# Gathered keys and queries turned at group 12 instead of 2, and batch 1's values loaded straight into their tile

## The chip, the cores and the metric

The kernel runs on one core of one Trainium2 chip. The time is what the device takes for one execution, in microseconds (us). The engines named here: PE (TensorE) does matrix products, and PEld is its loading of weights; DVE (VectorE) and ACT (ScalarE) work on tiles; POOL (GpSimd) makes small copies and issues those DMAs that also change the data's type; SP (SyncE) issues the other DMAs. Each engine takes its instructions in the order in which the program gives them, so an instruction that waits holds up all that is behind it on its engine.

## The reference

Eight batches, eight heads, 576 positions, heads of 64. Each query sees the keys within 32 positions; 8 given global positions are seen by all and see all. The attention's output, one row of 512 per position, goes through two layers with a "snake" between them.

```python
scores = scale * np.matmul(q, k.transpose(0, 1, 3, 2))
mask = np.abs(pos[:, None] - pos[None, :]) <= window
mask = mask | is_global[:, None] | is_global[None, :]
attn = softmax(np.where(mask, scores, -1e9))
x = (attn @ v).transpose(0, 2, 1, 3).reshape(B * S, H * D)
h = x @ w_in
g = h + np.sin(alpha * h) ** 2 / (alpha + 1e-09)
out = g @ w_out
```

## The kernel before, in words

The work goes batch by batch, in an order written out by hand. For each batch there is an attention (`attention`, line 831) and a GEMM 1 with the snake (`gemm1`, line 1126); GEMM 2 of a batch (`gemm2`) is a queue of single products, from which `fill(n)` takes n at given places of the following attention and GEMM 1, so that PE has work there. The order is: attention 0, GEMM 1 of batch 0, attention 1 with GEMM 2 of batch 0 in it, GEMM 1 of batch 1, and so on.

**GEMM 1** has 16 groups (`nt`). Each takes 8 products of PE into one of three PSUM banks (zn, zr, zd in turn), then `sb` = sin on ACT (line 1187), its square `s2` on ACT (1190) or DVE (1192), and H on DVE (1193), which frees the bank. In GEMM 1 of batch 0, PE also turns batch 1's keys and queries head by head (`turn_lying`, groups 4, 7, 10 and 13, into the banks zo), and DVE and ACT put them in their places one group later (`place_lying`, groups 5, 8, 11 and 14, lines 685 and 692).

**The global keys and queries** of all batches are gathered by 16 small DMAs of SP (`gather_heads`, line 536), cast on POOL in group 1 (`cast_globals_kq`, line 766, first keys, then queries), turned by 32 small products of PE at the end of group 2 (`turn_kq`, line 775, into the bank zo1), and copied by DVE to kTg and qTg (line 780). In group 3 POOL issues the casts of batch 2's keys and queries to DRAM (`cast_qk(2)`, line 337) and copies the globals of batch 1 into its key and query tiles (`place_globals`, three copies, lines 378 and 381), which attention 1's scores read.

**The values** of batches 0 and 1 lie in the tiles VF0 and VF1: two halves of partitions, each with even rows and, from a copy (`odd_rows`, line 415), odd rows beside them; `edge_tiles` (line 421) makes the tile VE of the rows at the edge, two copies for each half. A batch's numerators (`numerators`, products with VF and VE at line 911) need both. Batch 0's values come by 12 DMAs of POOL (line 396) straight from the input. Batch 1's come in two steps: POOL casts them into a DRAM tile `vpd` with one DMA (line 402), and SP loads VF1 from it with two (line 408). For batch 1, POOL makes odd_rows and edge_tiles of the second half in group 3 and DVE those of the first in attention 1.

**POOL's queue** in the beginning, DMAs and casts in order: keys and queries of batch 0, the 12 of values 0, w_in's first half, the cast of the gathered values, keys and queries of batch 1 (first heads), w_in's second half, keys and queries of batch 1 (last heads), w_out's first half, vpd, w_out's second half, the casts of `cast_globals_kq`, and then `cast_qk(2)`.

**Attention 1** goes over four head pairs (`hp`). Each has two halves of scores (line 863), exp on ACT (871) and a mask on DVE (`cover`, 880); `denominators(hp - 1)`, whose logarithm (ACT) comes before the sums GD (DVE, line 805); from hp 2 on `numerators(hp - 2)`, normalised on DVE (954). ACT loads a table for exp at its start (line 838) and one for sin at its end (1031). After each head pair, `beside(hp)` adds work: for batch 1 at 0 the value copies on DVE, `turn_qk(2)` (two transposing DMAs of SP, line 354, from the casts of `cast_qk(2)`), and at 0 and 1 the squares of the batch before (`square_x`, lines 1070 to 1074). `beside(-1)` comes before the first head pair, `beside(4)` after the last has been normalised.

**Batch 2's keys and queries**, once transposed, go to their tiles in eight copies of DVE (`place`, lines 370 and 363), four of keys first; for batch 2 all eight are made in groups 4, 5, 7, 8, 10, 11, 13 and 14 of GEMM 1 of batch 1. For later batches they are made in the attention, in `beside(2)`, `(3)` and `(4)`.

Of the kernel before, what the change touches and what calls it, by code (L numbers as in the profile page):

```python
# [12 lines left out]
DT = mybir.dt  # L13
# [237 lines left out]
def kernel(  # L251
# [11 lines left out]
    nc = tc.nc  # L263
    B, H, S, D = q.shape
# [7 lines left out]
    NH = KT // 2  # L272
    CT = DM // P
    NT = DFF // P
    HALF = S // 2
# [13 lines left out]
    dramp = mctx.enter_context(tc.tile_pool(name="dramp", bufs=2, space=bass.MemoryType.DRAM))  # L289
# [38 lines left out]

    cast = {}
    turned = {}  # L330
    vpd = dramp.tile([HALF, H, 2, D], DT.bfloat16, name="vpd")

    def cast_qk(b):

# [55 lines left out]
            tensor=q0.tensor, offset=q0.offset, ap=[list(q0.ap[0]), [2 * QROW, NHP], [SEG, 7], [1, 4]]  # L390
        )

    def load_v0():
        for half in range(2):
            for m in range(NT6):
                nc.gpsimd.dma_start(
                    out=VF[0][half * D : half * D + NH, m].rearrange("p h y d -> p h (y d)"),
                    in_=v[0].rearrange("h (n m a y) d -> n m a h (y d)", n=2, a=NH, y=2)[half, m],
                )

    def cast_v1():
        nc.gpsimd.dma_start(
            out=vpd[:].rearrange("s h y d -> s h (y d)"), in_=v[1].rearrange("h (s y) d -> s h (y d)", y=2)
        )

    def load_v1():
        for half in range(2):
            nc.sync.dma_start(
                out=VF[1][half * D : half * D + NH].rearrange("p m h y d -> p m (h y d)"),
                in_=vpd[:].rearrange("(n m a) h y d -> n a m (h y d)", n=2, a=NH)[half],  # L410
            )

    def odd_rows(b, half, copy):
        r = half * D
        copy(out=VF[b][r + 32 : r + 32 + NH, :, :, 0], in_=VF[b][r : r + NH, :, :, 1])

    def edge_tiles(b, half, copy):
        r, m = (1 - half) * D, half * (NT6 - 1)
        for y in range(2):
            o = half * D + y * 32  # L420
            copy(out=VE[b][o : o + NH], in_=VF[b][r : r + NH, m, :, y])
# [94 lines left out]
    for t in (gidx8, gp64):  # L516
        nc.vector.memset(t[:].bitcast(DT.int32), 0)
    nc.sync.dma_start(
        out=g64[:],
# [114 lines left out]
        nc.gpsimd.iota(qpos[half * D : half * D + D], pattern=[[KT, NT6], [1, 2], [2, 24]], base=half * HALF,  # L634
                       channel_multiplier=0, allow_small_or_imprecise_dtypes=True)
    gather(v, gv)
    load_v0()
    load_w_in((0,))
    nc.gpsimd.tensor_copy(out=VGb[:], in_=gv.rearrange("p h d -> p (h d)"))
    for hps in (early, late):  # L640
# [2 lines left out]
        if hps == early:  # L643
            load_w_in((1,))
    load_w_out((0,))
    cast_v1()
    load_w_out((1,))
    gather_heads(k, gk)
    gather_heads(q, gq)
# [414 lines left out]
    def square_x(b, part):  # L1064


        W = SG if b == B - 1 else S
        xf = xTs[b][:, :, 0:W]
        if part == 0:
            nc.vector.tensor_tensor(out=SQ[:, :, 0:W], in0=xf, in1=xf, op=ALU.mult)  # L1070
            return
        nc.vector.tensor_tensor(out=SQ[:, 0:2, 0:W], in0=SQ[:, 0:2, 0:W], in1=SQ[:, 2:4, 0:W], op=ALU.add)
        nc.vector.tensor_tensor(out=SQ[:, 0, 0:W], in0=SQ[:, 0, 0:W], in1=SQ[:, 1, 0:W], op=ALU.add)
        nc.vector.tensor_tensor(out=RM[:, 0:W], in0=RM[:, 0:W], in1=SQ[:, 0, 0:W], op=ALU.max)
# [45 lines left out]
    ON_ACT_FIRST = (1, 3, 5, 7, 9, 11, 13, 14)  # L1120
    ON_ACT_SECOND = (1, 3, 5, 7, 9, 10, 12, 13)

    TURNED, PLACED, GLOBALS = (4, 7, 10, 13), (5, 8, 11, 14), 2
    PLACED_LATE = {4: 0, 5: 1, 7: 2, 8: 3, 10: 4, 11: 5, 13: 6, 14: 7}

    def gemm1(b):


        while len(waiting) > 1:
            fill(1)  # L1130
        xT = xTs[b]
        r0 = (b % 2) * S
        more = b == B - 1
        W = SG if more else S
        hr = tc.alloc_tile_pool(name="hr", bufs=1, space=PSUM)
        hs = {}

        def chunks(nt, cs, parts=slice(0, 2)):
            if nt not in hs:
                hs[nt] = (zn, None, zd)[nt % 3] or hr.tile([P, 2, 512], DT.float32, name="zr")  # L1140
            h = hs[nt]
            for c in cs:
                for h_part, lo, hi in halves(h, W)[parts]:
                    nc.tensor.matmul(  # L1144
                        out=h_part, lhsT=w_in[:, c, nt * P : (nt + 1) * P], rhs=xT[:, c, lo:hi],
                        start=(c == 0), stop=(c == CT - 1), skip_group_check=True,
                    )

        on_act = (ON_ACT_FIRST, ON_ACT_SECOND, ON_ACT)[min(b, 2)]
        for nt in range(NT):  # L1150
            at_group[0] = (b, nt)
            if b == 1 and nt in PLACED_LATE:
                place(2, *PLACES[PLACED_LATE[nt]], nc.vector.tensor_copy)
            if b == 0 and nt in PLACED:
                hp = PLACED.index(nt)
                for w, copy in ((1, nc.vector.tensor_copy), (0, nc.scalar.copy)):
                    place_lying(1, w, hp, banks_of[NHP - 1][w], copy)
            if b == 0 and nt == 1:
                lay_global_values(1, zo[0], nc.vector.tensor_copy)
                cast_globals_kq()  # L1160
            if b == 0 and nt == GLOBALS + 1:

                cast_qk(2)
                load_v1()
                for part in range(3):
                    place_globals(1, part, nc.gpsimd.tensor_copy)
                odd_rows(1, 1, nc.gpsimd.tensor_copy)
                edge_tiles(1, 1, nc.gpsimd.tensor_copy)
            if more and nt == SOON:
                put_globals(slice(0, SOON))  # L1170
            if nt == 0:

                for n in range(2):
                    chunks(n, range(CT - 1), slice(0, 2 - more))
                for n in range(2 * more):
                    chunks(n, range(CT - 1), slice(1, 2))
            chunks(nt, range(CT - 1, CT) if nt < 2 else range(CT))
            h = columns(hs[nt], W)
            fill((GROUP_LAST if more else PER_GROUP)[nt])
            if nt and copied[0] == (b, nt - 2):  # L1180
                fill(AFTER_COPY)
            if b == 0 and nt in TURNED:
                turn_lying(1, TURNED.index(nt), banks_of[NHP - 1])
            if b == 0 and nt == GLOBALS:
                turn_kq()
            sb = spool.tile([P, SG], DT.bfloat16, name="sb")
            nc.scalar.activation(out=sb[:, 0:W], in_=h, func=AF.Sin, scale=alphaT[:, nt : nt + 1])  # L1187
            s2 = spool.tile([P, SG], DT.bfloat16, name="s2")
            if nt in on_act:
                nc.scalar.activation(out=s2[:, 0:W], in_=sb[:, 0:W], func=AF.Square)  # L1190
            else:
                nc.vector.tensor_tensor(out=s2[:, 0:W], in0=sb[:, 0:W], in1=sb[:, 0:W], op=ALU.mult)  # L1192
            nc.vector.scalar_tensor_tensor(  # L1193
                out=H2[:, nt, r0 : r0 + W], in0=s2[:, 0:W], scalar=recipT[:, nt : nt + 1], in1=h,
                op0=ALU.mult, op1=ALU.add,
            )
        hr.release()
        at_group[0] = None
# [121 lines left out]
    def places_at(b_att, at):  # L1320
        if b_att + 1 == B:
            return ()
        share = {} if b_att == 1 else {2: (0, 3), 3: (3, 6), 4: (6, 8)}
        return PLACES[slice(*share.get(at, (0, 0)))]

    def phase_a(b_att, b_moe):
        def beside(at):

            if b_att == 0:
                copy = nc.vector.tensor_copy  # L1330
                if at in (0, 2):
                    hp = 2 + at // 2
                    turn_lying(0, hp, banks_of[hp])
                    place_lying(0, 1, hp, banks_of[hp][1], copy)
                    place_lying(0, 0, hp, banks_of[hp][0], nc.scalar.copy)
                if at == 1:
                    set_recip()
                if at == 3:
                    lay_global_values(0, zo[0], nc.scalar.copy)
                return  # L1340
            if b_att == 1 and at == 0:
                odd_rows(1, 0, nc.vector.tensor_copy)
                edge_tiles(1, 0, nc.vector.tensor_copy)
            if b_att in (3, 4) and at == -1:
                find_columns(b_att - 3)
            if at == 2 and b_att == B - 1:
                global_rows(slice(0, B - 1))
            if b_att == 5 and at == 3:
                load_columns()
            if 0 <= at < 2:  # L1350
                square_x(b_moe, at)
            if at == 2 and 1 < b_att and b_att + 2 < B:
                pace(xTs[b_att][0:1, 0, 0:1])
                cast_qk(b_att + 2)
                cast_v(b_att + 2)
            if b_moe == 0 and at == 0:
                turn_qk(2)
            for which, t, y in places_at(b_att, at):
                place(b_att + 1, which, t, y, nc.vector.tensor_copy)

        if b_moe is not None:
            waiting.append(gemm2(b_moe))
        attention(b_att, beside)
# [70 lines left out]
```

## Time and profile before

| | |
|---|---|
| time, median of 3 runs | 352.59 us (352.12 to 353.14) |
| profiled execution, its own time | 353.27 us |
| its span, first to last instruction | 351.6 us |
| mean granted PE clock | 0.988 |
| busy: PE, DVE, ACT, POOL | 320.5, 274.1, 283.5, 60.9 us |
| chain that ended last: PE, DVE, issue, ACT, SP's queue, DMA | 69%, 9%, 6%, 5%, 5%, 4% |

A row of a timeline gives the start and the length in us, then engine, line, operation, output and inputs, shapes and count; the bracket gives how long the engine was idle just before and what ended that. DMA issues stand under the engine that issues them, with the time of issuing and not of the transfer; the transfer's time to landing is in the answers on DMAs. The chain of waits is followed back from the last instruction, at each step to what released it.

### The profile page before, as it was taken

The numbers are of one execution on the slowest core, as the hardware profiler recorded it, in microseconds if no ns is written. First come the engines' busy times: TensorE is split into PE (matmuls) and PEld (weight loads), VectorE is DVE, ScalarE is ACT, GpSimd is POOL, SyncE is SP. The second block draws the span as 40 slices with busy tenths as digits, with TensorE's granted clock in tenths as the row PEclk, the third lists the DMA queues.
The fourth block names the chain that finished last, engine by engine and source line by source line (L and its number), as shares of the span: only waits on it lengthen the run. The fifth ranks groups of instructions, "written<-read, shape, count | busy, mean of one in ns | idle before, by whom it ended". The sixth has DMA issues, their size and how long they took to land.

```text
span 351.6 us, 11665 instructions
## 1 busy us (share of the span) xinstructions
PE 320.5 (91%) x4851; PEld 203.3 (58%) x4851; DVE 274.1 (78%) x531; ACT 283.5 (81%) x411; POOL 60.9 (17%) x91
## 2 busy tenths in 40 slices
PE   0786799799899899999999999999999999999993
PEld 0644575366655575567656665577557755665543
DVE  5875488958989788887888787978797788788930
ACT  9876398877888888989898889989898888888611
POOL 7971302900004000310013000400000000002600
PEclk9999699999999999999999999999999999999999
DMA  7999999899194938499629991791724111010232
GB/s 103 117 182 206 200 225 198 112 212 181 37 165 77 209 76 166 99 178 180 101 64 176 195 121 62 152 187 41 176 64 96 30 32 63 5 31 2 76 91 66
DMA packets 80333, 41.79 MB, mean 119 GB/s; under 512 B 65442, under 2 KB 74002, under 8 KB 79890
## 3 DMA queue, kind: packets, MB, share of 16 engines
q0 software_dynamic: 38912, 18.50, 41.4%
q1 hardware_dynamic: 41362, 22.48, 29.7%
q8 instruction: 39, 0.64, 0.8%
q14 instruction: 20, 0.16, 0.2%
HBM read 41.85 MB, written 20.77 MB: 178 GB/s over the span
## 4 chain that ended last, share of the span: by engine, by line
PE 69%; DVE 9%; issue 6%; ACT 5%; SPq 5%; DMA 4%; POOL 0%; DVEq 0%; ACTq 0%; POOLq 0%
PE zo L1245 29%; PE zn L1144 12%; PE zr L1144 10%; PE zd L1144 10%; PE ring L863 3%; DVE H L1193 2%; DMA SQ<-in_k_dram 2%; DMA SQ<-in_q_dram 2%; ACT sb L1187 2%; SPq L542 2%; PE zn L911 2%; PE zd L911 1%; DVE QX L363 1%; SPq L536 1%; SPq L532 1%
## 5 line engine op out<-in xcount | busy, mean ns | idle before, releaser
L1245 PE MATMUL zo<-w_out,H 128*128 128x512 bf16 (+1 forms) x576 | 147.1, 377 | 0.4 <-DVE KX L685 0.4
L1144 PEld LDWEIGHTS <-w_in 128*128 128x128 bf16 x1024 | 100.4, 98 | 48.4 <-issue 12.8
L1245 PEld LDWEIGHTS <-H 128*128 128x128 bf16 x592 | 53.7, 98 | 46.5 <-issue 0.6
L1144 PE MATMUL zn<-xT,w_in 128*128 128x288 bf16 (+1 forms) x384 | 57.9, 290 | 3.6 <-DVE GN L805 2.7
L1187 ACT ACTIVATE sb<-zn,alphaT 128x576 bf16<-128x576 f32 (+1 forms) x48 | 35.6, 742 | 19.9 <-PE zn L1144 19.6
L1144 PE MATMUL zr<-xT,w_in 128*128 128x288 bf16 x320 | 48.9, 291 | 0.9 <-issue 0.7
L1193 DVE SCALAR_TENSOR_TENSOR H<-s,recipT,zn 128x576 bf16<-128x576 bf16 (+1 forms) x48 | 39.5, 822 | 10.9 <-ACT s L1190 7.6
L1144 PE MATMUL zd<-xT,w_in 128*128 128x288 bf16 x320 | 46.6, 289 | 1.0 <-DVE H L1193 0.9
L871 ACT ACTIVATE E<-ring 128x720 bf16<-128x720 f32 x46 | 35.8, 779 | 10.8 <-PE ring L863 10.0
L1190 ACT ACTIVATE s<-sb 128x576 bf16<-128x576 bf16 (+1 forms) x58 | 40.0, 689 | 1.8
L880 DVE TENSOR_TENSOR E<-E,MASKT 128x720 bf16<-128x720 bf16 x64 | 35.6, 564 | 6.8 <-ACT E L871 4.9
L1192 DVE TENSOR_TENSOR s<-sb 128x576 bf16<-128x576 bf16 (+1 forms) x70 | 32.0, 458 | 11.3 <-ACT sb L1187 11.0
L1193 DVE SCALAR_TENSOR_TENSOR H<-s,recipT,zd 128x576 bf16<-128x576 bf16 (+1 forms) x40 | 32.9, 822 | 8.4 <-ACT s L1190 6.0
L1193 DVE SCALAR_TENSOR_TENSOR H<-s,recipT,zr 128x576 bf16<-128x576 bf16 (+1 forms) x40 | 32.9, 822 | 5.2 <-ACT s L1190 3.6
L1187 ACT ACTIVATE sb<-zd,alphaT 128x576 bf16<-128x576 f32 (+1 forms) x40 | 29.6, 739 | 6.1 <-PE zd L1144 5.4
L1187 ACT ACTIVATE sb<-zr,alphaT 128x576 bf16<-128x576 f32 (+1 forms) x40 | 29.6, 740 | 4.4 <-PE zr L1144 4.3
L1252 ACT COPY osb<-zo 128x512 f32<-128x512 f32 (+1 forms) x36 | 20.9, 580 | 12.1 <-PE zo L1245 8.5
L863 PEld LDWEIGHTS <-KX 64*64 64x64 bf16 x896 | 15.8, 112 | 20.3 <-issue 19.5
L348 POOL COPY seen<-xT 1x1 bf16<-1x1 bf16 x4 | 1.9, 478 | 138.6 <-DVE GN L805 138.6
L828 ACT ACTIVATE R<-L,shift 128x576 f32<-128x576 f32 x32 | 24.9, 781 | 0.4
L1235 POOL COPY H<-H 128x11 bf16 (+1 forms) x16 | 7.2, 452 | 98.7 <-DVE H L1193 97.9
L863 PE MATMUL ring<-QX,KX 64*64 64x120 bf16 (+2 forms) x644 | 17.2, 219 | 1.7 <-ACT QX L692 0.7
(181 smaller groups left out, 364.4 us busy)
## 6 DMA issues: line engine op xcount, KB each, us to landing
VF<-vd SPq DMA_DIRECT2D x24, 168.0 KB
kd<-in_k_dram POOLq DMA_DIRECT2D x6, 576.0 KB, 6.2
qd<-in_q_dram POOLq DMA_DIRECT2D x6, 576.0 KB, 10.1
vd<-in_v_dram POOLq DMA_DIRECT2D x6, 576.0 KB, 17.9
w_in<-in_moe_w_in_dram POOLq DMA_DIRECT2D x2, 1024.0 KB, 12.0
w_out<-in_moe_w_out_dram POOLq DMA_DIRECT2D x2, 1024.0 KB, 22.8
out_dram<-osb SPq DMA_DIRECT2D x7, 256.0 KB
out_dram<-osb SPq DMA_DIRECT2D x8, 224.0 KB
```

Source lines behind the costliest of these rows:

```text
L828: nc.scalar.activation(out=R[:], in_=L[:], func=AF.Exp, scale=-1.0, bias=shift[:, 0:1])
L863: nc.tensor.matmul(out=z[half * D : (half + 1) * D, t, 0 : G3 * WCOL].rearrange("p (m x c) -> p m x c", x=2, c=60)[:, m % G3, :, c0:c1], l ...
L871: nc.scalar.activation(out=weights(hp, g), in_=z[:, :, 0 : G3 * WCOL], func=AF.Exp, scale=scale)
L880: nc.vector.tensor_tensor(out=Eg, in0=Eg, in1=MASKT[:, None, G3 * g : G3 * (g + 1), :].rearrange("p o m c -> p o (m c)").to_broadcast([P, ...
L911: nc.tensor.matmul(out=nd(hp, key)[t * D : (t + 1) * D, half, :, a - half * CUT : z - half * CUT], lhsT=ones[rows, 0:D] if key else values ...
L1144: nc.tensor.matmul(out=h_part, lhsT=w_in[:, c, nt * P : (nt + 1) * P], rhs=xT[:, c, lo:hi], start=(c == 0), stop=(c == CT - 1), skip_group ...
L1187: nc.scalar.activation(out=sb[:, 0:W], in_=h, func=AF.Sin, scale=alphaT[:, nt : nt + 1])
L1190: nc.scalar.activation(out=s2[:, 0:W], in_=sb[:, 0:W], func=AF.Square)
L1192: nc.vector.tensor_tensor(out=s2[:, 0:W], in0=sb[:, 0:W], in1=sb[:, 0:W], op=ALU.mult)
L1193: nc.vector.scalar_tensor_tensor(out=H2[:, nt, r0 : r0 + W], in0=s2[:, 0:W], scalar=recipT[:, nt : nt + 1], in1=h, op0=ALU.mult, op1=ALU.add,)
L1245: nc.tensor.matmul(out=ops[:, cols], lhsT=H2[:, nt, blk * P : (blk + 1) * P], rhs=w_out[:, nt, cols], start=(nt == 0), stop=(nt == NT - 1) ...
L1252: nc.scalar.copy(out=osb[:, cols], in_=ops[:, cols])
```

## The change

`turn_kq` moves from group 2 to group 12 of GEMM 1 of batch 0, and `cast_qk(2)` and the three copies of globals from group 3 to group 13 with it. `cast_globals_kq` stays in group 1. The values of batch 1 come as those of batch 0 do, by 12 DMAs of POOL, at the place where `cast_v1` stood; the tile vpd and SP's two DMAs go. POOL's odd_rows and edge_tiles go to DVE: odd_rows of the first half before the first head pair of attention 1, of the second half after it, all four edge copies after the second. `square_x` of that attention moves from after head pairs 0 and 1 to after 2 and 3. Of batch 2's eight copies two of keys go to attention 1's end, and six stay in GEMM 1 of batch 1, in groups 4, 6, 8, 10, 12 and 13.

```diff
-    vpd = dramp.tile([HALF, H, 2, D], DT.bfloat16, name="vpd")
...
-    def load_v0():
+    def load_values(b):
         for half in range(2):
             for m in range(NT6):
                 nc.gpsimd.dma_start(
-                    out=VF[0][half * D : half * D + NH, m].rearrange("p h y d -> p h (y d)"),
-                    in_=v[0].rearrange("h (n m a y) d -> n m a h (y d)", n=2, a=NH, y=2)[half, m],
+                    out=VF[b][half * D : half * D + NH, m].rearrange("p h y d -> p h (y d)"),
+                    in_=v[b].rearrange("h (n m a y) d -> n m a h (y d)", n=2, a=NH, y=2)[half, m],
                 )
-
-    def cast_v1():
...
-    def load_v1():
...
-    load_v0()
+    load_values(0)
...
-    cast_v1()
+    load_values(1)
     load_w_out((1,))
...
-    TURNED, PLACED, GLOBALS = (4, 7, 10, 13), (5, 8, 11, 14), 2
-    PLACED_LATE = {4: 0, 5: 1, 7: 2, 8: 3, 10: 4, 11: 5, 13: 6, 14: 7}
+    TURNED, PLACED, GLOBALS = (4, 7, 10, 13), (5, 8, 11, 14), 12
+    PLACED_LATE = {4: 2, 6: 3, 8: 4, 10: 5, 12: 6, 13: 7}
...
             if b == 0 and nt == GLOBALS + 1:
-
                 cast_qk(2)
-                load_v1()
                 for part in range(3):
                     place_globals(1, part, nc.gpsimd.tensor_copy)
-                odd_rows(1, 1, nc.gpsimd.tensor_copy)
-                edge_tiles(1, 1, nc.gpsimd.tensor_copy)
...
-        share = {} if b_att == 1 else {2: (0, 3), 3: (3, 6), 4: (6, 8)}
+        share = {4: (0, 2)} if b_att == 1 else {2: (0, 3), 3: (3, 6), 4: (6, 8)}
...
-            if b_att == 1 and at == 0:
-                odd_rows(1, 0, nc.vector.tensor_copy)
-                edge_tiles(1, 0, nc.vector.tensor_copy)
+            if b_att == 1 and at < 2:
+                if at < 1:
+                    odd_rows(1, at + 1, nc.vector.tensor_copy)
+                else:
+                    for half in range(2):
+                        edge_tiles(1, half, nc.vector.tensor_copy)
...
-            if 0 <= at < 2:
-                square_x(b_moe, at)
+            part = at - 2 if b_att == 1 else at
+            if 0 <= part < 2:
+                square_x(b_moe, part)
```

More of the change, by code (lines that the diff above doesn't have):

```diff
@@ L396, in load_v0 @@
                 nc.gpsimd.dma_start(
-                    out=VF[0][half * D : half * D + NH, m].rearrange("p h y d -> p h (y d)"),
-                    in_=v[0].rearrange("h (n m a y) d -> n m a h (y d)", n=2, a=NH, y=2)[half, m],
-                )
-    def cast_v1():
-        nc.gpsimd.dma_start(
-            out=vpd[:].rearrange("s h y d -> s h (y d)"), in_=v[1].rearrange("h (s y) d -> s h (y d)", y=2)
-        )
-    def load_v1():
[L407 to L411, printed above, removed]
+                    out=VF[b][half * D : half * D + NH, m].rearrange("p h y d -> p h (y d)"),
+                    in_=v[b].rearrange("h (n m a y) d -> n m a h (y d)", n=2, a=NH, y=2)[half, m],
+                )
     def odd_rows(b, half, copy):
```

## Prediction

> **What bounds the kernel now.** The chain of waits is mostly TensorE's work in its order, so I read where TensorE stands still in the first two batches. First its timeline (start, length, engine, line, operation, count; in brackets the idle time before and what ended it), with one row of attention 2 to compare.
>
> ```profile
> 36.94 0.61 PE L775 MATMUL zo<-identb,gkq 64*64 64x32 bf16 x16 [4.82 <-POOL gkq L766]
> 37.48 2.10 PE L1144 MATMUL zn<-xT,w_in 128*128 128x288 bf16 x8
> ...
> 43.51 1.14 PE L1144 MATMUL zn<-xT,w_in 128*128 128x288 bf16 x8
> ...
> 51.00 1.14 PE L1144 MATMUL zn<-xT,w_in 128*128 128x288 bf16 x8
> ...
> 54.84 1.14 PE L1144 MATMUL zn<-xT,w_in 128*128 128x288 bf16 x8
> ...
> 58.41 2.33 PE L1245 MATMUL zo<-w_out,H 128*128 128x512 bf16 x10
> ...
> 62.99 0.35 PE L911 MATMUL zd<-E,ones 56*64 56x120 bf16 x16 [1.65 <-DVE E L880]
> ...
> 65.30 0.46 PE L911 MATMUL zn<-E,VF 56*64 56x88 bf16 x24
> ...
> 105.32 0.48 PE L911 MATMUL zn<-E,VF 56*64 56x88 bf16 x28
> ```
>
> Two stalls: 4.82 us in group 2 of GEMM 1 of batch 0, where turn_kq waits for the cast of the gathered queries, and 1.65 us in attention 1. The four zn rows of L1144 are groups 3, 6, 12 and 15. The table of windows (busy time of PE, PEld, DVE, ACT, POOL; then granted clock) shows a second price of the first stall.
>
> ```profile
> 32.60:36.00 3.40, 0.00 (x0) 0.00 (x0) 0.83 (x2) 0.10 (x1) 0.00 (x0) 1.00 1.17 207
> 36.00:39.40 3.40, 2.46 (x25) 1.72 (x26) 1.77 (x4) 0.00 (x0) 2.41 (x5) 0.51 1.23 205
> 39.40:42.80 3.40, 3.40 (x60) 2.18 (x59) 1.44 (x3) 2.60 (x4) 0.67 (x3) 0.50 1.46 197
> ```
>
> One wholly idle window, then two at 0.51 and 0.50. Groups 3 to 5 took 43.51 - 37.48 = 6.03 us; groups 6 to 14 took 54.84 - 43.51 = 11.33 us, 3.78 for three with one turn of batch 1's heads. The slow clock cost 6.03 - 3.78 = 2.25 us.
>
> What delays such a cast is GpSimd's queue. Its timeline, and answers on single DMAs (KB, us from issue to landing: w_in's halves issued at 16.41 and 20.69, w_out's first half issued at 23.18):
>
> ```profile
> 9.09 7.34 POOL L396 DMA_DIRECT2D VF<-in_v_dram  x12
> 16.41 0.80 POOL L450 DMA_DIRECT2D w_in<-in_moe_w_in_dram  x1
> ...
> 20.69 0.78 POOL L450 DMA_DIRECT2D w_in<-in_moe_w_in_dram  x1
> ...
> 23.18 0.96 POOL L456 DMA_DIRECT2D w_out<-in_moe_w_out_dram  x1
> 24.13 1.36 POOL L402 DMA_DIRECT2D vpd<-in_v_dram  x1
> 26.44 0.90 POOL L456 DMA_DIRECT2D w_out<-in_moe_w_out_dram  x1 [0.95 <-DMA w_in<-in_moe_w_in_dram]
> ...
> 36.28 0.61 POOL L766 CAST gkq<-SQ 64x512 bf16<-64x512 f32 x1 [6.46 <-DMA SQ<-in_q_dram]
> 36.84 0.53 POOL L337 DMA_DIRECT2D kd<-in_k_dram  x1
> ...
> 38.58 0.85 POOL L378 COPY KX<-kTg 128x384 bf16<-128x384 bf16 x1 [0.71 <-DVE qTg L780]
> 39.38 0.69 POOL L381 COPY QX<-qTg 128x112 bf16<-128x112 bf16 x2
> 59.57 2.98 POOL L415 COPY VF<-VF 24x3072 bf16<-24x3072 bf16 x1 [19.51 <-DMA VF<-vpd]
> ```
> ```profile
> w_in<-in_moe_w_in_dram POOLq DMA_DIRECT2D x1, 1024.0 KB, 9.7
> ...
> w_in<-in_moe_w_in_dram POOLq DMA_DIRECT2D x1, 1024.0 KB, 14.3
> ...
> w_out<-in_moe_w_out_dram POOLq DMA_DIRECT2D x1, 1024.0 KB, 20.3
> ```
>
> The 0.95 us before 26.44 matters most. That DMA needs nothing of w_in, yet waited for w_in's first half, which landed at 16.41 + 9.7 = 26.1 and is the eighth DMA before it on this queue (keys, queries, w_in, keys, queries, w_out, vpd lie between). I take it that each DMA of GpSimd waits for the one eight before it to land, and then starts 0.3 us later.
>
> **The change: turn_kq at group 12, and 12 DMAs in place of one.** Group 3 starts when its bank is free:
>
> ```profile
> 31.30 0.81 DVE L1193 SCALAR_TENSOR_TENSOR H<-s,recipT,zn 128x576 bf16<-128x576 bf16 x1
> ```
>
> That is 32.1. Nine groups at 11.33 us bring group 12 to 43.4 and its matmuls' end to 44.5 (w_in's second half, due at group 8, has landed at 20.69 + 14.3 = 35.0; group 8 starts at 38.4).
>
> GpSimd is later than that. Piece 5 of the values waits for w_in's second half (35.0), piece 8 for w_out's first half: 23.18 + 20.3 = 43.5, so it starts at 43.8. Pieces 8 to 12 take 7.34 / 12 = 0.61 each: 46.9. w_out's second half, 0.90: 47.8. Only then come the two casts, 0.61 each; with 0.3 us for the waits in front, the keys' ends at 48.7 and the queries' at 49.3. The gathers have long landed. TensorE idles from 44.5 to 48.7, 4.2 us, and ends turn_kq at 49.3 + 0.61 = 49.9. Before, group 12's matmuls ended at 52.0; from there to attention 1 all is the same, so attention 1 starts 52.0 - 49.9 = **2.1 us** earlier. Bounds: 2.9 (no lag, and ScalarE, which has caught up, takes the last groups faster) and 0.3 (each of the six issues 0.3 slower). In the stall the VectorE copies of kTg and qTg wait, and behind them H of group 12, for which group 15's bank waits: that is in the 5.3 us from 52.0 to the table load below.
>
> After the casts GpSimd issues the casts of batch 2 (0.53 each) and makes the three copies of globals (0.85 + 0.69): 49.3 + 1.1 + 1.5 = 51.9, against attention 1's first scores at about 55. If that 3 us cover were gone, each us would count. On SyncE's queue, the transposes and what is behind them:
>
> ```profile
> 54.56 4.81 SPq L354 DMA_TRANSPOSE kt<-kd  x1
> ```
>
> Batch 2's keys are issued at 49.3 instead of 36.84, behind w_out's second half. That was issued at 46.9; 9.7 us (w_in's row) make it 56.6; GEMM 2 first needs it at its 17th product, the last of the ten of the row at 58.41, at some 60 before and 58 after. The transpose can then start at 57 to 60 instead of 54.56; its readers are the copies at attention 1's end, near 75. Behind it wait the logarithm and output stores, whose buffers have room: nothing, unless keys came 10 us later.
>
> **Attention 1 without GpSimd's copies, with them on VectorE.** VectorE's rows by line (shortest, median, longest ns), its timeline, and ScalarE's table loads, which bound attentions 1 and 2:
>
> ```profile
> L880 DVE TENSOR_TENSOR E<-E,MASKT x64: 469/529/2861, 13.0 to 297.3; 128x720 bf16<-128x720 bf16 x64
> ```
> ```profile
> L415 DVE COPY VF<-VF x3: 954/1124/1254, 18.9 to 63.0; 24x3072 bf16<-24x3072 bf16 x3
> ```
> ```profile
> L421 DVE COPY VE<-VF x4: 282/298/585, 23.1 to 64.9; 24x512 bf16<-24x512 bf16 x4
> ```
> ```profile
> L370 DVE COPY KX<-kt x24: 442/455/459, 84.4 to 261.4; 64x1152 bf16<-64x1152 bf16 x24
> ```
> ```profile
> 59.42 3.52 DVE L880 TENSOR_TENSOR E<-E,MASKT 128x720 bf16<-128x720 bf16 x2 [0.61 <-ACT E L871]
> ...
> 105.72 0.23 DVE L805 TENSOR_REDUCE GD<-zd 128x8 f32<-128x64 f32 x1 [0.78 <-ACT L L821]
> ```
> ```profile
> 57.32 1.28 ACT L838 ACT_TABLE_LOAD   x1
> ...
> 76.99 1.28 ACT L1031 ACT_TABLE_LOAD   x1
> ...
> 98.67 1.28 ACT L838 ACT_TABLE_LOAD   x1
> ...
> 115.16 1.28 ACT L1031 ACT_TABLE_LOAD   x1
> ```
>
> Two masks took 3.52 us beside GpSimd's 2.98 us copy, where two take 1.06: 2.46 are freed. VectorE gains one odd_rows (1.12) and two edge copies (0.60): net 0.74. By the other way: attention 2 reaches its first sums (GD) 7.3 us after its table load; four edge copies (1.2) put attention 1's first numerators at 8.5, where they stood at 65.30 - 57.32 = 8.0 (6.65 in attention 2). From there attention 2 needs 115.16 - 105.32 = 9.84, attention 1 needed 76.99 - 65.30 = 11.69; the squares moved behind take the place of attention 2's key and query copies, and the products of the global values add some 0.5: 18.8 against 19.67, 0.8 gained. I take **0.8**; bounds -0.1 (1.65 of idle, 1.72 added) and 2.5 (all that is freed).
>
> **Keys of batch 2.** Two copies of 0.455 us leave GEMM 1 of batch 1 for attention 1's end, where VectorE has nothing during the 1.28 us table load. At best 0.9, at worst 0 (TensorE bounds these groups): **0.5**.
>
> Sum: 2.1 + 0.8 + 0.5 = 3.4. The profiled execution took 353.27 us, so 349.9; the median of the runs shown, 352.59, is 0.7 lower, so **349.2**.
>
> **Rivals.**
>
> *The slow clock returns.* An idle 4.2 us holds one whole 3.4 us window in (4.2 - 3.4) / 3.4, a quarter, of its positions. The rows above put the next windows at 42.8 to 46.2 and 46.2 to 49.6, neither empty, but the grid need not stand so again. Price 2.25: 351.4. Chance 0.2. [...]
>
> *The wait vanishes.* If GpSimd's DMAs don't wait for the eighth before, the casts end near 37 and group 15 starts at 32.1 + 15.1 + 0.6 for turn_kq, 47.8 instead of 54.84: 7.0 in place of 2.1, 344.3. Against it stands the row at 26.44. Chance 0.1.
>
> *GpSimd comes later still (slower).* The same DMA took twice as long at its slowest:
>
> ```profile
> L480 POOL DMA_DIRECT2D H<-in_q_dram x4: 587/660/1184, 2.4 to 22.0; - x4
> ```
>
> With 0.6 more for each of pieces 8 to 12 and w_out, turn_kq ends 3.5 us later, at 53.4, 1.4 later than before, and the idle 7.7 us holds a whole window for certain. The other gains of 1.3 remain: 352.59 + 1.4 + 2.25 - 1.3 = 354.9. With the slow clock it is a loss once the casts end 1.2 us later than forecast, past 50.5. Against it: VectorE, which could hinder GpSimd, is idle in the stall too, and the twelve issues at 9.09 ran at 0.61. Chance 0.18. [...]
>
> **How the numbers follow.** Forecast 0.52, slow clock 0.2, vanished wait 0.1, later still 0.18. The forecast's own bounds give 346.3 to 352.4 (gains of 6.3 and 0.2, 0.7 taken off). The range, 345.5 to 353.5, holds these and the slow clock, and the nearer part of the other two, whose prices may come in part; what it leaves out I put at 0.07 below and 0.1 above. No change is within 0.3%, 1.1 us, about what a measurement can tell. Faster: the forecast, the vanished wait and half of the slow clock, 0.72; same 0.13; slower 0.15.
>
> **What would show it.** Right: no wait in group 2; a wait of 3 to 5 us at L775 after group 12, ended by the cast; GpSimd's eighth piece starting at about 43.8, the casts at 48 to 49; clock 1.00 through 32 to 43; masks of attention 1 near 0.53 each; numerators about 8.5 us after the table load. Wrong: casts before 44, a stall at attention 1's first scores for the globals, or the transposes late for the copies at its end.

## The result and the profile after

| | before | changed |
|---|---|---|
| median of 10 runs each, in turn on one chip | 353.16 us (352.12 to 358.17) | 350.45 us (348.03 to 350.86) |
| ratio, 95% interval | | 0.992 (0.9897 to 0.9942) |
| profiled execution: own time, span | 353.27, 351.6 us | 350.85, 349.2 us |
| from the span's start to sin's table, at attention 0's end | 28.05 | 29.17 |
| GEMM 1 of batch 0, to exp's table | 29.27 | 28.91 |
| attention 1, to sin's table | 19.67 | 17.59 |
| GEMM 1 of batch 1 | 21.68 | 21.67 |
| attention 2 | 16.48 | 16.00 |

Faster by 2.7 us in the medians; 349.2 was forecast. A run more than 1.5% above the fastest of its kernel, as the one at 358.17, is left out of the ratio. The stages are cut at ScalarE's table loads, which alternate between exp and sin. The stages behind attention 2 agree within 0.1 us, except the last one, from attention 7's end to the end of the span: 50.98 and 50.31.

First, TensorE around group 12 and in attention 1 of the changed kernel, in the columns of the rows before:

```profile
44.87 1.14 PE L1131 MATMUL zn<-xT,w_in 128*128 128x288 bf16 x8
49.97 1.17 PE L762 MATMUL zo<-identb,gkq 64*64 64x32 bf16 x32 [3.95 <-POOL gkq L753]
51.07 2.10 PE L1131 MATMUL zr<-xT,w_in 128*128 128x288 bf16 x8
...
53.88 2.06 PE L1131 MATMUL zd<-xT,w_in 128*128 128x288 bf16 x8
55.77 1.15 PE L1131 MATMUL zn<-xT,w_in 128*128 128x288 bf16 x8
...
63.92 0.46 PE L898 MATMUL zn<-E,VF 56*64 56x88 bf16 x24
65.17 0.20 PE L898 MATMUL zn<-E,VE 56*64 56x32 bf16 x2 [0.79 <-DVE VE L408]
```

The wait of group 2 is gone and stands at group 12, 3.95 us where 4.2 were forecast. The two groups behind it took 2.10 and 2.06 us, the group in front and the last one 1.14 and 1.15. GpSimd in the same time:

```profile
22.25 0.90 POOL L443 DMA_DIRECT2D w_out<-in_moe_w_out_dram  x1
...
37.87 0.61 POOL L395 DMA_DIRECT2D VF<-in_v_dram  x1 [5.53 <-DMA w_in<-in_moe_w_in_dram]
...
45.35 3.02 POOL L395 DMA_DIRECT2D VF<-in_v_dram  x5 [4.12 <-DMA w_out<-in_moe_w_out_dram]
48.36 0.90 POOL L443 DMA_DIRECT2D w_out<-in_moe_w_out_dram  x1
49.30 1.17 POOL L753 CAST gkq<-SQ 64x512 bf16<-64x512 f32 x2
```

This is the queue that the prediction drew: a piece of the values held until w_in's second half has landed, pieces 8 to 12 held until w_out's first half has, and behind them, with nothing else between, w_out's second half and the two casts. The table of windows (us, busy PE, PEld, DVE, ACT, POOL; granted clock, DMA share, GB/s) on the same grid as before:

```profile
42.80:46.20 3.40, 3.22 (x70) 2.24 (x67) 2.92 (x5) 3.34 (x6) 0.85 (x2) 1.00 0.96 85
46.20:49.60 3.40, 0.00 (x0) 0.00 (x0) 1.28 (x2) 0.96 (x2) 3.36 (x6) 0.90 0.80 73
49.60:53.00 3.40, 3.03 (x40) 2.05 (x40) 1.79 (x4) 0.00 (x0) 3.12 (x6) 0.50 0.96 114
```

The clock falls to half at the wait, here too. The trace's own record of the clock puts that at 48.94 to 55.77, 6.83 us. Between its first rise and its last fall, at the end, the stretches of that record are 23.89, 6.83 and 293.55 us long here, and 13.65, 6.83 and 307.20 in the kernel before: each a multiple of 3.413 us within 0.03. So I lay windows of 3.41 us on its edges. The window before this fall held a little work:

```profile
45.53:48.94 3.41, 0.49 (x4) 0.15 (x2) 1.95 (x3) 1.60 (x3) 3.41 (x6) 1.00 0.62 55
```

Then VectorE in attention 1, with no GpSimd copy beside it:

```profile
59.60 0.95 DVE L402 COPY VF<-VF 24x3072 bf16<-24x3072 bf16 x1
60.58 0.98 DVE L867 TENSOR_TENSOR E<-E,MASKT 128x720 bf16<-128x720 bf16 x2
...
64.28 0.23 DVE L792 TENSOR_REDUCE GD<-zd 128x8 f32<-128x64 f32 x1 [0.73 <-ACT L L808]
64.54 1.20 DVE L408 COPY VE<-VF 24x512 bf16<-24x512 bf16 x4
...
76.53 0.91 DVE L369 COPY KX<-kt 64x1152 bf16<-64x1152 bf16 x2
```

Two masks take 0.98 us instead of 3.52, the first odd_rows 0.95, the four edge copies 1.20 together, and the two key copies at the end 0.91 without a wait.

### The profile page after: what moved, and what is told of

Read it like the earlier page. It is cut to its first block, busy times and chain, and to the rows that moved or that the text cites. A ratio compares the mean times of both kernels' runs of the same rounds, so it can differ in the third digit from the quotient of the medians.

```text
span 349.2 us, 11618 instructions
## 1 busy us (share of the span) xinstructions
PE 313.5 (90%) x4791; PEld 203.1 (58%) x4851; DVE 273.7 (78%) x534; ACT 283.4 (81%) x411; POOL 62.0 (18%) x99
## 4 chain that ended last, share of the span: by engine, by line
PE 68%; DMA 8%; DVE 7%; issue 6%; ACT 5%; SPq 4%; POOL 2%; POOLq 0%; DVEq 0%; ACTq 0%
PE zo L1228 29%; PE zn L1131 12%; PE zr L1131 10%; PE zd L1131 9%; DMA w_out<-in_moe_w_out_dram 7%; PE ring L850 3%; DVE H L1176 2%; SPq L529 2%; PE zd L898 1%; DVE QX L362 1%; PE zn L898 1%; ACT L L808 1%; ACT sb L1170 1%; SPq L519 1%; ACT s L1173 1%
## 5 line engine op out<-in xcount | busy, mean ns | idle before, releaser
L1228 PE MATMUL zo<-w_out,H 128*128 128x512 bf16 (+1 forms) x516 | 134.0, 376 | 6.0 <-issue 5.2
L1131 PE MATMUL zn<-xT,w_in 128*128 128x288 bf16 (+1 forms) x384 | 57.0, 287 | 5.0 <-DVE GN L792 3.1
L1175 DVE TENSOR_TENSOR s<-sb 128x576 bf16<-128x576 bf16 (+1 forms) x70 | 32.7, 467 | 10.2 <-ACT sb L1170 9.9
L867 DVE TENSOR_TENSOR E<-E,MASKT 128x720 bf16<-128x720 bf16 x64 | 33.8, 536 | 6.6 <-ACT E L858 4.6
```

Source lines behind the costliest of these rows:

```text
L867: nc.vector.tensor_tensor(out=Eg, in0=Eg, in1=MASKT[:, None, G3 * g : G3 * (g + 1), :].rearrange("p o m c -> p o (m c)").to_broadcast([P, ...
L1131: nc.tensor.matmul(out=h_part, lhsT=w_in[:, c, nt * P : (nt + 1) * P], rhs=xT[:, c, lo:hi], start=(c == 0), stop=(c == CT - 1), skip_group ...
L1228: nc.tensor.matmul(out=ops[:, cols], lhsT=H2[:, nt, blk * P : (blk + 1) * P], rhs=w_out[:, nt, cols], start=(nt == 0), stop=(nt == NT - 1) ...
```

## The experiments

Two theories stood against each other. Theory one, the prediction's: the time is GpSimd's queue (each of its DMAs waits for the eighth before it) and VectorE's freed time; the slow clock is a price that falls only on a wholly idle window. The rival: the clock, and not the queue, takes most of what the move of turn_kq should bring. A third question was which part carries the gain at all.

**The move alone.** On the kernel before, one constant: turn_kq goes to group 12, and what stands behind it (the casts of batch 2, SP's loads from vpd, the globals and GpSimd's value copies) to group 13.

```diff
-    TURNED, PLACED, GLOBALS = (4, 7, 10, 13), (5, 8, 11, 14), 2
+    TURNED, PLACED, GLOBALS = (4, 7, 10, 13), (5, 8, 11, 14), 12
```

> The kernel before with turn_kq at group 12 and cast_qk(2) and the globals at 13; batch 1's values still go by the DRAM tile, GpSimd still copies them. Theory A (GpSimd's DMAs wait for the one eight before; in the change the twelve pieces keep GpSimd from its casts until 50 us): here the casts end near 37, TensorE doesn't wait in group 12, the clock stays 1.00 to 50 us, and attention 1's table load stands near 51 instead of 57.3. Part is given back in attention 1, where GpSimd's copies wait for the tile: 347 to 350 us in all. Rival B (the casts are late through the DMA traffic of that time, not through the pieces; the change gains in attention 1 alone): the wait at group 12 is as long as in the changed kernel, 352 to 353 us.

Measured: 352.8 us (10 runs, 351.45 to 354.42) against 352.82, ratio 0.9993 (0.9967 to 1.0018). No gain. The time is the one that B gave, but not B's mechanism: there is no wait at group 12, as A had it. The stages say where it went: GEMM 1 of batch 0 took 22.73 instead of 29.27, attention 1 24.39 instead of 19.67, and attention 0 was longer by 2.7 (30.73; see the last section). TensorE:

```profile
47.52 0.68 PE L775 MATMUL zo<-identb,gkq 64*64 64x32 bf16 x32
...
63.26 0.48 PE L911 MATMUL zn<-E,VF 56*64 56x88 bf16 x22 [3.60 <-POOL VF L415]
...
65.60 0.24 PE L911 MATMUL zn<-E,VE 56*64 56x32 bf16 x2 [1.87 <-POOL VE L421]
```

The casts had been made at 28.70 and 35.71. But attention 1 starts 3.9 us sooner (exp's table at 53.46 for 57.32), and its values don't come sooner: SP issued the two loads from vpd at 46.05, where the kernel before has 46.77. VectorE waits for both, and GpSimd's copies of the second half, at 60.43 and 63.26, end after the first numerators are due:

```profile
57.98 0.95 DVE L415 COPY VF<-VF 24x3072 bf16<-24x3072 bf16 x1 [1.23 <-DMA VF<-vpd]
60.31 3.04 DVE L421 COPY VE<-VF 24x512 bf16<-24x512 bf16 x2 [1.38 <-DMA VF<-vpd]
```

Two edge copies of VectorE took 3.04 us beside GpSimd's 2.77 for odd_rows. Behind the stall of 3.60 us the clock was halved, from 63.91 to 70.74. So the move took 6.5 us out of the stage where it is made, of which this run had lost 2.7 in attention 0, and gave 4.7 back at the next late thing, the values. By itself it brings nothing in the total. No run has the move with vpd kept and the copies on VectorE, so what the 12 pieces themselves bring at group 12 is not shown.

**The pieces alone, turn_kq at group 2.** On the kernel before, the 12 DMAs in vpd's place.

```diff
...
-    cast_v1()
+    load_values(1)
     load_w_out((1,))
...
```

> The kernel before with batch 1's values in twelve DMAs straight into their tile, and nothing else: turn_kq stays at group 2, GpSimd's value copies stay. A: the casts come at 49 to 50 us as in the changed kernel, so group 2 waits some 13 us longer than in the kernel before: about 365 us. B: the casts wait only for the gathers and the issues (12 x 0.61 against 1.36, 6 us more), and end at 37 to 40: 353 to 356 us.

Measured: one run, 363.74 us. TensorE, and GpSimd's queue:

```profile
48.21 1.16 PE L762 MATMUL zo<-identb,gkq 64*64 64x32 bf16 x32 [16.66 <-POOL gkq L753]
```
```profile
43.60 3.01 POOL L395 DMA_DIRECT2D VF<-in_v_dram  x5 [4.32 <-DMA w_out<-in_moe_w_out_dram]
46.60 0.91 POOL L443 DMA_DIRECT2D w_out<-in_moe_w_out_dram  x1
47.55 1.16 POOL L753 CAST gkq<-SQ 64x512 bf16<-64x512 f32 x2
```

The wait for the eighth DMA before is shown: a piece that needs nothing of w_out starts when w_out has landed, after 4.32 us of idle time, and the casts behind it end 11.8 us later than before (48.71 for 36.89). Whether the chip makes this wait or the program as it was built asks for it, no run here separates. At group 2 the 12 pieces cost TensorE a wait of 16.66 us.

**The value copies on VectorE alone.** On the kernel before, with vpd kept; the squares move as in the change.

```diff
-                odd_rows(1, 1, nc.gpsimd.tensor_copy)
-                edge_tiles(1, 1, nc.gpsimd.tensor_copy)
...
-            if b_att == 1 and at == 0:
-                odd_rows(1, 0, nc.vector.tensor_copy)
-                edge_tiles(1, 0, nc.vector.tensor_copy)
+            if b_att == 1 and at < 2:
+                if at < 1:
+                    odd_rows(1, at + 1, nc.vector.tensor_copy)
+                else:
+                    for half in range(2):
+                        edge_tiles(1, half, nc.vector.tensor_copy)
...
-            if 0 <= at < 2:
-                square_x(b_moe, at)
+            part = at - 2 if b_att == 1 else at
+            if 0 <= part < 2:
+                square_x(b_moe, part)
```

> The kernel before with the value copies of batch 1 on VectorE instead of GpSimd, and the squares of attention 1 after head pairs 2 and 3, as in the change; nothing else. A: the two masks of 3.52 us become 1.06, attention 1 between its table loads takes 17.6 us as in the changed kernel instead of 19.67: 2.0 us, 351.2. My forecast for this part was 0.8 gained (352.4). B (all of the change's gain is here): 350.5.

Measured: 351.59 us (12 runs) against 352.82, ratio 0.9962 (0.9938 to 0.9985). Attention 1 took 17.96 instead of 19.67: 1.7 by the copies and the squares together. The changed kernel had 17.59 there, and 17.93 and 17.76 in two more profiled runs (below), so nearly all of its gain in this stage is this part. The masks there:

```profile
59.70 0.98 DVE L880 TENSOR_TENSOR E<-E,MASKT 128x720 bf16<-128x720 bf16 x2
```

**The casts first, the pieces around them.** On the changed kernel, so that the casts don't stand behind w_out.

```diff
     load_w_out((0,))
-    load_values(1)
     load_w_out((1,))
+    load_values(1, range(3))
...
                 cast_globals_kq()
+                load_values(1, range(3, 7))
             if b == 0 and nt == GLOBALS + 1:
-                cast_qk(2)
                 for part in range(3):
                     place_globals(1, part, nc.gpsimd.tensor_copy)
+                load_values(1, range(7, 12))
+                cast_qk(2)
```

> The changed kernel with GpSimd's order altered: w_out's second half and pieces 1 to 3, then the casts of the gathered keys and queries, pieces 4 to 7, and in group 13 the globals, pieces 8 to 12 and only then the casts of batch 2. A: the casts end near 38 us, no wait in group 12, clock 1.00, attention 1's table load near 51.5 instead of 58.1; the later pieces and casts have cover: 343 to 346 us. B: the wait at group 12 stays, 350 to 351 us. If pieces 8 to 12 come too late for attention 1, the wait shows there at VectorE's odd rows, and the gain is smaller: 347 to 349.

Measured: 345.35 us (6 runs, 344.22 to 351.1), ratio 0.9759 (0.9726 to 0.9793); it beats both kernels. GpSimd's queue, and turn_kq:

```profile
30.88 0.61 POOL L753 CAST gkq<-SQ 64x512 bf16<-64x512 f32 x1
35.88 0.61 POOL L753 CAST gkq<-SQ 64x512 bf16<-64x512 f32 x1 [4.39 <-DMA LC<-L]
...
43.42 0.61 POOL L395 DMA_DIRECT2D VF<-in_v_dram  x1 [4.06 <-DMA w_out<-in_moe_w_out_dram]
...
71.35 2.75 POOL L343 DMA_DIRECT2D vd<-in_v_dram  x1
```
```profile
46.17 0.68 PE L762 MATMUL zo<-identb,gkq 64*64 64x32 bf16 x32
```

The casts are done ten us before group 12, TensorE doesn't wait there, the clock keeps its speed, and GEMM 1 of batch 0 takes 23.20 (28.91 in the changed kernel). One thing was lost: GEMM 1 of batch 1 took 22.85 instead of 21.67. VectorE's two key copies at attention 1's end met GpSimd's issue of the row at 71.35:

```profile
71.33 3.05 DVE L369 COPY KX<-kt 64x1152 bf16<-64x1152 bf16 x2
```

3.05 us where the changed kernel shows 0.91.

**Work in the wait of group 12.** On the changed kernel, 12 products of ones by ones ahead of turn_kq, and beside it the changed kernel itself.

```diff
+                warm(zo[1], 12)
                 turn_kq()
```

> The changed kernel with twelve extra products of ones with ones (128x512, into bank zo1, their result used by nothing) in front of turn_kq in group 12, where TensorE waits 3.95 us for the cast. They take some 2.6 us of the wait and change nothing else. Theory C (the clock halves because the window was nearly idle, 0.47 us of work in 3.41, and that costs groups 13 to 15 and the turn some 2.2 us): clock 1.00 through 46 to 56, mean over 0.994, and 350.45 - 2.2 = 348.2 us, what the one run with mean clock 0.995 took (348.03). Rival D (the slow clock is hidden, since VectorE and ScalarE set the pace of the last groups): 350.4, no change.

> The changed kernel once more, unaltered, as a measure beside the other kernels of this call: 350.4 us, and in the profile a table load for attention 1 near 57.5 to 58.5 with the clock at 0.5 before it.

Measured: 348.93 us with the products (6 runs, 347.31 to 349.72), 349.01 without (7 runs, 348.4 to 350.99). As a comparison of times this is inconclusive, for two reasons that the traces show. With the products, the clock still fell for one window, 51.07 to 54.49; the window before it held 1.39 us of work:

```profile
47.66:51.07 3.41, 1.39 (x36) 0.77 (x35) 0.00 (x0) 0.00 (x0) 3.37 (x6) 1.00 0.79 78
```
```profile
50.08 0.98 PE L762 MATMUL zo<-identb,gkq 64*64 64x32 bf16 x32 [1.89 <-POOL gkq L753]
```

And in the profiled run of the unaltered kernel the clock didn't fall at all, since there was hardly a wait. The clock had first risen at 32.90 us there, 25.05 in the profile further up, so attention 0 and the first groups ran slowly and TensorE ended group 12 at 48.48 instead of 46.01; and the casts began 1.1 us sooner.

```profile
48.88 0.98 PE L762 MATMUL zo<-identb,gkq 64*64 64x32 bf16 x32 [0.39 <-POOL gkq L753]
```

So the changed kernel comes out in more than one way. Of its 23 runs in all, the six with a mean clock of 0.994 or more have a median of 348.4 us (347.6 to 349.24), the other seventeen, at 0.990 or less, 350.4 (348.53 to 351.6). The two overlap, and only three of these runs have a profile; in those, the wait is long or short by when TensorE gets to group 12 and when the casts come.

**The same, with 19 products,** which last until the casts are done, again beside the changed kernel.

```diff
+                warm(zo[1], 19)
                 turn_kq()
```

> The changed kernel with 19 products of ones by ones (0.229 us each by the row of twelve at 45.44, 2.75 us) in the wait of group 12, so that TensorE idles there for about 0.3 us instead of 3.95 and no window of 3.4 us is nearly empty. Theory C, the slow clock is a price of its own, about 2.0 us: the clock stays at 1.00 after its first rise, turn_kq's start to attention 1's table load takes 6.1 us (as in the copy of the changed kernel whose clock stayed up) instead of 8.11, and the run is 2.0 us under a copy of the changed kernel whose clock drops. Theory D, what the slow clock costs comes out of time in which TensorE would have waited anyway: that stretch stays at 7.5 us or more.

> The changed kernel once more, beside the run above. With the clock halved after the wait of group 12: about 350.4 and 8.1 us from turn_kq's start to the table load; with the clock kept: about 348.4 and 6.1 us.

Measured: 347.51 us (6 runs, 346.91 to 348.31; 0.9833 of before, 0.9803 to 0.9862) against 349.68 (6 runs, 347.6 to 351.6; 0.9897, 0.9856 to 0.9938). TensorE's and ScalarE's rows of the run with the products:

```profile
45.13 4.26 PE L588 MATMUL zo<-ones 128*128 128x512 bf16 x19
49.32 0.68 PE L762 MATMUL zo<-identb,gkq 64*64 64x32 bf16 x32
```
```profile
55.12 1.28 ACT L825 ACT_TABLE_LOAD   x1
```

And of the changed kernel beside it:

```profile
49.36 1.17 PE L762 MATMUL zo<-identb,gkq 64*64 64x32 bf16 x32 [4.18 <-POOL gkq L753]
```
```profile
57.51 1.28 ACT L825 ACT_TABLE_LOAD   x1
```

turn_kq starts within 0.04 us of the same time, and exp's table is loaded 55.12 - 49.32 = 5.80 us later in the one and 57.51 - 49.36 = 8.15 in the other. The profiled runs differ by 349.74 - 347.30 = 2.44. In these rows the products change nothing but the clock, which stayed at 1.00 from 24.54 on in the one and was halved from 48.80 to 55.63 in the other: the slow clock costs 2.35 us, theory C. The ratios of the two kernels differ less clearly than that, since some runs of the changed kernel keep the clock by themselves (347.6 us at 0.997).

**The keys alone.** On the kernel before, two of batch 2's key copies at attention 1's end.

```diff
-    PLACED_LATE = {4: 0, 5: 1, 7: 2, 8: 3, 10: 4, 11: 5, 13: 6, 14: 7}
+    PLACED_LATE = {4: 2, 6: 3, 8: 4, 10: 5, 12: 6, 13: 7}
...
-        share = {} if b_att == 1 else {2: (0, 3), 3: (3, 6), 4: (6, 8)}
+        share = {4: (0, 2)} if b_att == 1 else {2: (0, 3), 3: (3, 6), 4: (6, 8)}
```

> The kernel before with only the move of the eight copies of batch 2: two of keys to attention 1's end, six in groups 4, 6, 8, 10, 12, 13. My forecast was 0.5 us gained in GEMM 1 of batch 1. By the trace of the changed kernel it is 0 there (21.67 between the table loads against 21.68) and 0.5 in attention 2 (16.00 against 16.48), since VectorE's last copy ends a group earlier: 352.3. If the copies give nothing at all: 352.8.

Measured: 352.7 us (12 runs, 351.37 to 358.12) against 352.91, ratio 1.0 (0.9971 to 1.003): the total can't tell it. The table loads can:

```profile
77.28 1.28 ACT L1031 ACT_TABLE_LOAD   x1
98.75 1.28 ACT L838 ACT_TABLE_LOAD   x1
114.72 1.28 ACT L1031 ACT_TABLE_LOAD   x1
```

GEMM 1 of batch 1 takes 21.47 and attention 2 15.97, where before had 21.68 and 16.48. The half us comes, but most of it in the attention behind.

**The casts first, with the old places of the keys,** so that VectorE's copies don't meet GpSimd at attention 1's end. The edit is that of the casts first, with PLACED_LATE and share as in the kernel before.

> e4_casts_first with the eight copies of batch 2 where the kernel before has them (groups 4 to 14 of GEMM 1 of batch 1). In e4 the two at attention 1's end took 3.05 us beside GpSimd's issue of batch 3's values (2.75 us), and GEMM 1 of batch 1 took 22.85 instead of 21.68. If that meeting is the cause: 21.7 there, attention 2 back at 16.5, 0.7 us gained in all, 344.6. If not: GEMM 1 of batch 1 stays at 22.8 and the time is 345.8.

Measured: 345.37 us (6 runs, 344.34 to 346.23), ratio 0.9791 (0.9761 to 0.982), where 344.6 was expected. GEMM 1 of batch 1 is back at 21.87, so the meeting was its price. But attention 2 is back at 16.49, and attention 1 took 20.39. In that run attention 1 started 2.1 us sooner than with the casts first (49.97 for 52.12) and the last pieces only 0.65 sooner, so VectorE waited for them, and behind a window that was half empty the clock was halved:

```profile
55.57 0.95 DVE L402 COPY VF<-VF 24x3072 bf16<-24x3072 bf16 x1 [2.13 <-DMA VF<-in_v_dram]
```
```profile
56.92:60.33 3.41, 1.72 (x29) 0.68 (x17) 3.27 (x10) 1.78 (x3) 0.00 (x0) 1.00 1.00 185
60.33:63.74 3.41, 3.41 (x52) 1.60 (x51) 1.46 (x3) 2.12 (x4) 0.00 (x0) 0.50 1.43 203
```

**The casts first, w_out's second half behind the fourth piece, all eight key copies early.** On the version with the casts first.

```diff
     load_w_out((0,))
-    load_w_out((1,))
     load_values(1, range(3))
...
-    PLACED_LATE = {4: 2, 6: 3, 8: 4, 10: 5, 12: 6, 13: 7}
+    PLACED_LATE = {3: 0, 4: 1, 6: 2, 8: 3, 10: 4, 11: 5, 12: 6, 13: 7}
...
-                load_values(1, range(3, 7))
+                load_values(1, range(3, 4))
+                load_w_out((1,))
+                load_values(1, range(4, 11))
...
-                load_values(1, range(7, 12))
+                load_values(1, range(11, 12))
...
-        share = {4: (0, 2)} if b_att == 1 else {2: (0, 3), 3: (3, 6), 4: (6, 8)}
+        share = {} if b_att == 1 else {2: (0, 3), 3: (3, 6), 4: (6, 8)}
```

> The two casts first on GpSimd's queue as in the 345.35 us version, the second half of w_out behind the fourth piece of the values, so that the pieces 8 to 11 no longer wait for it, and all eight key copies of batch 2 in groups 3 to 13 of GEMM 1 of batch 1, none at attention 1's end. If VectorE's 3.05 us meeting and the late pieces were the two prices left: GEMM 1 of batch 1 back at 21.7 (from 22.85), attention 2 at 16.0 (16.49 with late keys), attention 1 at 18.0 or less (18.36 and 20.39), so 345.35 - 1.2 - 0.4 = 343.8. If w_out's second half, issued some 10 us later, comes late for GEMM 2 of batch 0, TensorE waits for it in attention 1 and that stage is over 20 us: 346 or more.

Measured: 345.72 us (6 runs, 345.26 to 345.94), ratio 0.9778 (0.975 to 0.9806); the 343.8 hoped for did not come. Attention 2 took 16.00 as expected, attention 1 18.41 as in the version with the casts first, and GEMM 1 of batch 1 22.26 instead of 21.7. TensorE waits there for VectorE's H in four groups, 1.59 us in all; these are the last two:

```profile
88.27 1.14 PE L1130 MATMUL zd<-xT,w_in 128*128 128x288 bf16 x8 [0.65 <-DVE H L1179]
89.60 1.14 PE L1130 MATMUL zn<-xT,w_in 128*128 128x288 bf16 x8 [0.19 <-DVE H L1179]
```

The kernel before, with the same eight copies in other groups, waits 1.47 us there and takes 21.68, so these waits explain at most 0.1 us; the other half us stays open.

The three versions with the casts first stand at 345.35, 345.37 and 345.72. They can't be told apart by these runs.

## Why the prediction was right or wrong

**GpSimd's queue: right.** The eight-DMA wait, the cover that it eats, and the place of the new wait came as drawn; the run with the pieces at group 2 shows the rule by itself, with 16.66 us of wait. All of it came somewhat later: the pieces 8 to 12 at 45.35 for 43.8, the casts' end at 50.47 for 49.3, turn_kq's end at 51.14 for 49.9. What set that is w_out's first half: it was issued sooner, at 22.25 for 23.18, but held the pieces until 45.35, so it took some 2.5 us longer than in the kernel before; why is not shown. TensorE came 1.5 us later as well, its group 12 ending at 44.87 + 1.14 = 46.01 for 44.5, of which 1.12 us are attention 0's later end in this run. No row ties the one delay to the other, so it is luck that the wait, 3.95 for 4.2, fits so well. Counted from sin's table load, turn_kq's end is at 51.14 - 29.17 = 21.97 us where the forecast had 49.9 - 28.05 = 21.85.

**The slow clock: wrong, and the largest error.** The step that failed is "The rows above put the next windows at 42.8 to 46.2 and 46.2 to 49.6, neither empty", and from it the chance of 0.2 for the rival. The size of that rival, 2.25, was right (2.35 measured). Its condition was wrong twice. The windows didn't stand on the grid of the kernel before: the clock's record has an edge at 42.87 there and at 48.94 here, 6.07 us apart, which is no multiple of 3.41. And a window needn't be wholly idle: windows with 0.49, 1.39 and 1.72 us of work in 3.41 were followed by the slow clock here (in the second profiled run of the changed kernel in which it came, the window, 45.39 to 48.80, was wholly idle). The mean granted clock speaks for its having come in nine of the ten runs (0.986 to 0.990, 349.69 to 350.86 us); the tenth, at 0.995, took 348.03. What a window must hold stays open, and TensorE's busy time alone doesn't sort the windows: the kernel before has one with 1.76 us of work, and the run with the keys alone one with 1.69, less than the 1.72 above, and neither has the slow clock behind it.

```profile
59.94:63.35 3.41, 1.76 (x61) 1.07 (x60) 3.25 (x3) 2.29 (x4) 3.35 (x2) 1.00 1.19 170
```
```profile
60.08:63.49 3.41, 1.69 (x60) 0.93 (x58) 3.25 (x3) 2.37 (x4) 3.29 (x2) 1.00 1.21 186
```

**The term of 2.1 us** was thus right as far as turn_kq's end and lost behind it: from there to exp's table load 58.08 - 51.14 = 6.94 us instead of 5.3 (5.12 in the run with 19 products, whose clock stayed up). GEMM 1 of batch 0 gained 29.27 - 28.91 = 0.36 in the profiled pair. With the clock kept it took 26.46, a gain of 2.81, close to the upper bound of 2.9.

**Attention 1: right in direction, too small.** 0.8 was forecast, 2.08 came in the profiled pair, and 1.7 with the copies alone. The step that failed is "four edge copies (1.2) put attention 1's first numerators at 8.5". The first that need the edge copies stand at 65.17 - 58.08 = 7.1. Two things made it so. The sums GD were done 6.4 us after the table load and not 7.3, the figure of attention 2, which is 6.8 itself here, with the keys moved. And these products wait for the copies that they read and not for all four, which end at 65.74. The products with VF wait for none of them and stand at 63.92, 5.8 us after the load. The bound of 2.5, the time freed of masks, was nearer than the argument by attention 2.

**The keys: the size right, the place wrong.** 0.5 was forecast in GEMM 1 of batch 1, which stayed at 21.67. It came in attention 2, 16.00 for 16.48, and the run with the keys alone shows the same there (15.97). That the last copies in group 14 hold up attention 2's start is my reading; no run separates it.

**The sum.** 3.4 were forecast and 2.4 came in the profiled pair (2.7 in the medians): 2.35 lost to the clock, 1.3 more won in attention 1, and 0.6 more in GEMM 1 of batch 0 without the clock's part (0.36 + 2.35 for 2.1). The later attention 0 of that run took 1.1, and the last stage, which has none of the change in it, gave 0.7. That the total came near the number is luck: two errors, the clock and the size of attention 1, have opposite signs. By the prediction's own sum, the slow clock and casts that end at 50.5 would have left no gain; here they ended at 50.47 with the slow clock, and attention 1 carried the gain. With the clock kept the change gives 353.14 - 347.51 = 5.6 us, and with the casts first 7.5.

**The rivals.** That GpSimd would come later still did not happen: pieces 8 to 12 took 3.02 us, 0.60 each. The vanished wait did not happen either, but for the one profiled run in which TensorE came late by itself and 0.39 us was left; the wait for the eighth DMA was there too (4.41 us, until w_out's first half had landed).

## What to carry to other kernels

The wait that was moved here took with it the clock that it costs (half speed for 6.83 us at the old place and at the new one): before counting the gain of a move, ask whether the new wait can bring the slow clock (here 1.89 us of wait, with 1.39 us of work in the window, were enough), and whether that engine has cheap work to fill it. Count DMAs on GpSimd's queue, not their issue time: the casts of 0.6 us stood here behind DMAs that were held until the eighth DMA before them had landed (5.53 us for w_in's second half, 4.12 for w_out's first); put the short casts ahead of such DMAs (here 7.5 us under the kernel before instead of 2.7). And try a part alone before crediting it: the move of turn_kq gave nothing by itself.

## What the runs showed of the hardware

Attention 0, whose own work no kernel here alters, took from 27.46 to 30.73 us, and a later first rise of the clock stands with a longer one here: 28.05 with the rise at 22.39 us in the kernel before, and 28.55, 29.17 and 29.71 with the rise at 24.91, 25.05 and 32.90 in three profiled runs of the changed kernel. The rise has a part in whether TensorE comes early to group 12 and waits (its matmuls' end at 46.01 us and 3.95 of wait, with the rise at 25.05), or late and hardly does (48.48 and 0.39, with the rise at 32.90). What sets the rise is not shown.

VectorE's two copies took 3.05 us beside GpSimd's issue of one DMA (2.75 us, the row at 71.35) and 0.91 without it, as two masks took 3.52 us beside GpSimd's copy of 2.98 us and 0.98 without it. So in the run with the casts first an engine that only issued a transfer took 2.14 us of VectorE's time.
